# Attention and gated MLP in one kernel: the program is recorded first, then list-scheduled and pinned on each engine

## The chip, the cores and the metric

The kernel runs on one core of one Trainium2 chip. The metric is device time in microseconds (us); lower is better. The engines are TensorE (PE; its weight loads are PEld), VectorE (DVE), ScalarE (ACT), GpSimd (POOL) and SyncE (SP), which here issues every DMA.

## What is computed

Eight batches of 576 tokens. Each has eight attention heads of width 64, with a causal mask and a bias from a running sum; their outputs side by side are the input `x` (576 x 512) of a gated MLP that mixes along the sequence:

```python
bias   = -(cum[:, :, :, None] - cum[:, :, None, :])          # cum: cumsum of max(s, 0)
scores = where(causal, -1e9, scale * q @ k.T + minimum(bias, 0))
attn   = softmax(scores) @ v                                 # 64 heads
h = gelu(x @ w_in); u, v = halves of h                       # per batch, x from its 8 heads
v_n = layernorm(v) * g_ln
gated = u * (einsum('ts,bsd->btd', w_sg, v_n) + b_sg)
out = x + gated @ w_out
```

## The kernel before

All values are fp32, and most products are made from a rounded part and a remainder ("hi" and "lo", the helper `split`: a copy on ACT, then a subtraction on POOL or DVE). The first heads are left whole (8 for the scores, 12 for the product with v), since nothing fills TensorE there yet.

**A head** goes through `scores` (tiles `sc` in PSUM, two buffers; L297 and L298, L295 for whole heads), a masked running minimum on DVE (L305, into the SBUF tiles `p`, two sets for even and odd heads), the exponential on ACT (L315), `norm` on POOL (L338), 13 transposes on TensorE (`pt`, two buffers, L377), their evacuation into `pah`/`pal`, `pbh`/`pbl`, `pdh`/`pdl` (ACT copies at L88, DVE subtracts at L93), and the product with v (`xx`, one buffer, L450, and `x`, L472). ACT and DVE add the result's two halves into `xr` (L478, L479). Before a head starts, `split_head` makes `k1` and `k2` (ACT, POOL) and SP moves pieces of them by four DMAs.

**A batch's MLP**, `ffn`, first splits `xr` into `xs` (POOL, L90 and L93), four tiles, one per two heads. Its 29 units share three PSUM buffers: five `v` (tile `vm`, L510 and L524 to L527), eight `u` (`um`, L574), eight `s` (`sm`, L589 to L593), eight `o` (`om`, L608). A `v` unit ends in a chain over ACT, DVE and POOL (gelu, then layer norm). The input weights are prepared on the way, in `part`: tiles `wbits` (L216 to L222) and `wi`, `wo` (L88, L93).

**The order** is set twice. The code calls generators at places on a line that is counted in heads (`POS`, `F0`, `ORDER`); they are sorted, and the instructions are written in that order:

```python
    while steps:
        steps.sort()
        _, _, f, args = steps.pop(0)
        f(*args)
```

Then the tile framework (L711, `schedule_with_timeline_sim=True`) gives each instruction its place on its engine by a simulation of its own, and places the buffers. Each engine runs its list strictly in order.

Of the kernel before, what the change touches and what calls it, by code (L numbers as in the profile page):

```python
# [2 lines left out]

# [6 lines left out]
F32R = mybir.dt.float32r  # L10
# [3 lines left out]
AF = mybir.ActivationFunctionType  # L14
ALU = mybir.AluOpType
# [40 lines left out]
           wu=(7.0, 10.0), ws=(9.0, 11.0), wo=(11.0, 14.0), f0=2.0, f1=9.6)  # L56


@with_exitstack
def tile_attn_gmlp(  # L60
    ctx: ExitStack,
# [14 lines left out]
    att = ctx.enter_context(tc.tile_pool(name="att", bufs=2))  # L76
    moe = ctx.enter_context(tc.tile_pool(name="moe", bufs=1))
    ps_sc = ctx.enter_context(tc.tile_pool(name="ps_sc", bufs=2, space=bass.MemoryType.PSUM))
    ps_pt = ctx.enter_context(tc.tile_pool(name="ps_pt", bufs=2, space=bass.MemoryType.PSUM))
    ps_x = ctx.enter_context(tc.tile_pool(name="ps_x", bufs=1, space=bass.MemoryType.PSUM))  # L80
    ps_m = ctx.enter_context(tc.tile_pool(name="ps_m", bufs=3, space=bass.MemoryType.PSUM))

    def eng(key):
        return [{"s": nc.scalar, "g": nc.gpsimd, "v": nc.vector}[x] for x in ENG[key]]
# [11 lines left out]

    first = []

    def later():
        return tc.issue_after(first[0].ins)  # L100
# [24 lines left out]
    dram = ctx.enter_context(tc.tile_pool(name="dram", bufs=1, space=bass.MemoryType.DRAM))  # L125
# [52 lines left out]
    for i in range(2):  # L178
        t = const.tile([66, S], F32R, name=f"q2_{i}")
# [3 lines left out]
        for it in range(5):  # L183
            t = const.tile([P, PW[it]], F32, name=f"p_{i}_{it}")
# [4 lines left out]
        t = const.tile([P, 5], F32, name=f"sum_{i}")  # L189
# [36 lines left out]
    wide = w_in.dtype != F32  # L226
# [395 lines left out]
    steps = []  # L622
# [94 lines left out]
```

## Time and profile before

| | |
|---|---|
| median of 3 runs | 832.95 us (829.35 to 833.86) |
| profiled execution | 829.98 us, its span 828.2 us |
| granted TensorE clock, mean | 0.992 |
| PE busy | 794.3 us, 96% |
| DVE, ACT, POOL busy | 597.6, 577.4, 597.6 us, 70 to 72% |

Matmuls are pipelined: the duration of one runs over the start of the next, so a busy PE can still have been held up a little. Times of a chain are us from the span's start. A wait is put down to the engine whose semaphore came last.

### The profile page before, as it was taken

Reading aid. Unit: us, or ns where it says so; the run is one execution under the profiler, and the core shown is the slowest. Engines: PE = TensorE matmul, PEld = TensorE weight load, DVE = VectorE, ACT = ScalarE, POOL = GpSimd, SP = SyncE. Lnnn points to the kernel's source line nnn. Section 1 sums busy time; section 2 is a strip of 40 time slices with the busy share of each in tenths; the row PEclk is TensorE's granted clock in tenths of the full one; section 3 lists DMA queues with packets and bytes.
Section 4 is the critical chain, followed back from the end, with each engine's and each line's share of the span. In section 5 each row is a group of like instructions: output and inputs, shape, how many; then the busy total and the mean of one; then the engine's idle time right before and its main releaser. Section 6 shows DMA issues by size and latency. Waiting matters only on the chain.

```text
span 828.2 us, 16736 instructions
## 1 busy us (share of the span) xinstructions
PE 794.3 (96%) x5161; PEld 695.6 (84%) x5161; DVE 597.6 (72%) x1806; ACT 577.4 (70%) x1620; POOL 597.6 (72%) x979
## 2 busy tenths in 40 slices
PE   6899999899999999999999999999999999998898
PEld 3455666799989998999989997899989998997798
DVE  5995468975787678966887687965897678963552
ACT  4787778875686678867787677866887678853340
POOL 4987668888677767796778777796778778782541
PEclk9999999999999999999999999999999999999999
DMA  7656553334342453444434443444434443300001
GB/s 218 193 171 183 146 136 87 95 98 115 104 106 71 128 131 86 103 122 127 118 85 105 130 132 73 113 121 109 112 101 112 122 127 87 99 25 30 27 7 58
DMA packets 69804, 89.29 MB, mean 108 GB/s; under 512 B 25954, under 2 KB 42212, under 8 KB 69716
## 3 DMA queue, kind: packets, MB, share of 16 engines
q1 hardware_dynamic: 69716, 88.23, 40.6%
q8 instruction: 41, 0.67, 0.4%
q14 instruction: 47, 0.39, 0.2%
HBM read 42.27 MB, written 9.73 MB: 63 GB/s over the span
## 4 chain that ended last, share of the span: by engine, by line
PE 73%; DVE 13%; DMA 6%; ACT 3%; issue 3%; POOL 2%; SPq 1%; DVEq 0%; POOLq 0%; ACTq 0%
PE om L608 12%; PE sm L589 11%; PE um L574 10%; PE vm L510 9%; PE xx L450 9%; PE pt L377 8%; PE sc L297 4%; PE sc L298 4%; DVE p L305 2%; DMA q<-k 2%; PE sm L593 1%; DMA xq<-xs 1%; PE sm L592 1%; DVE vm L496 1%; DVE wbits L220 1%
## 5 line engine op out<-in xcount | busy, mean ns | idle before, releaser
L338 POOL TENSOR_SCALAR p<-p,rs 128x448 f32<-128x448 f32 (+4 forms) x372 | 181.0, 500 | 30.5 <-DVE rs L321 10.9
L315 ACT ACTIVATE p<-p,mn 128x448 f32<-128x448 f32 (+4 forms) x320 | 177.9, 557 | 25.5 <-DVE mn L305 23.4
L305 DVE CUSTOM_DVE_ANT_0 p<-sc,mask 64x64 f32<-64x64 f32 (+4 forms) x320 | 126.2, 422 | 55.3 <-PE pt L377 29.6
L377 PE MATMUL pt<-ident,p 128*128 128x128 f32 (+1 forms) x832 | 136.6, 278 | 4.6 <-DVE pbl L389 2.6
L574 PE MATMUL um<-xs,wi 128*128 128x288 f32 x768 | 124.1, 303 | 4.0 <-DVE vt L548 2.0
L589 PE MATMUL sm<-ws,vn 128*128 128x288 f32 x768 | 127.1, 300 | 0.4 <-DVE u L496 0.4
L93 POOL TENSOR_TENSOR k<-raw,k 128x576 fp32r<-128x576 f32 x56 | 80.6, 1439 | 63.7 <-ACT k L88 34.1
L608 PE MATMUL om<-gt,wo 128*128 128x288 f32 x768 | 125.6, 299 | 0.0
L574 PEld LDWEIGHTS um<-xs,wi 128*128 128x128 f32 x768 | 110.0, 191 | 10.3 <-DVE u L496 3.2
L377 PEld LDWEIGHTS pt<-ident,p 128*128 128x128 f32 (+1 forms) x832 | 97.0, 138 | 20.6 <-DVE pbl L389 5.4
L608 PEld LDWEIGHTS om<-gt,wo 128*128 128x128 f32 x768 | 110.5, 188 | 2.6 <-DVE ot L612 0.3
L589 PEld LDWEIGHTS sm<-ws,vn 128*128 128x128 f32 x768 | 109.9, 189 | 2.6 <-DVE u L496 1.5
L510 PE MATMUL vm<-wi,xs 128*128 128x512 f32 x384 | 105.5, 407 | 4.4 <-DVE u L496 2.2
L297 PE MATMUL sc<-k,q 128*128 128x448 f32 x336 | 100.7, 308 | 1.4 <-DVE mn L305 0.8
L298 PE MATMUL sc<-k,q 66*128 66x448 f32 x336 | 89.2, 298 | 0.4 <-DMA k<-cum 0.3
L88 ACT CAST pbh<-pt 128x512 fp32r<-128x512 f32 x104 | 49.0, 479 | 58.1 <-PE pt L377 58.0
L510 PEld LDWEIGHTS vm<-wi,xs 128*128 128x128 f32 x384 | 71.6, 194 | 20.8 <-DVE u L496 2.4
L93 POOL TENSOR_TENSOR gt<-u,gt 128x288 fp32r<-128x288 f32 x64 | 50.9, 807 | 44.3 <-ACT gt L88 43.9
L93 DVE TENSOR_TENSOR pbl<-pt,pbh 128x512 fp32r<-128x512 f32 x104 | 56.6, 549 | 16.8 <-ACT pbh L88 16.7
L297 PEld LDWEIGHTS sc<-k,q 128*128 128x128 f32 x336 | 60.6, 180 | 9.1 <-DVE mn L305 3.6
L298 PEld LDWEIGHTS sc<-k,q 66*128 66x128 f32 x336 | 60.7, 181 | 5.9 <-issue 0.8
L88 ACT CAST k<-raw 128x576 fp32r<-128x576 f32 x56 | 37.6, 671 | 38.8 <-PE sc L297 33.3
(142 smaller groups left out, 1703.2 us busy)
## 6 DMA issues: line engine op xcount, KB each, us to landing
q<-k SPq DMA_DIRECT2D x168, 144.0 KB
raw<-in_kq SPq DMA_DIRECT2D x56, 288.0 KB
vr<-in_vp SPq DMA_DIRECT2D x52, 192.0 KB
out_t<-ot SPq DMA_DIRECT2D x64, 144.0 KB
k<-k SPq DMA_DIRECT2D x56, 144.0 KB
wraw<-in_w_in SPq DMA_DIRECT2D x16, 256.0 KB
kf<-in_kq SPq DMA_DIRECT2D x8, 288.0 KB
qf<-in_kq SPq DMA_DIRECT2D x8, 288.0 KB
```

Of the source, the lines that this page charges most:

```text
L88: nc.scalar.copy(out=hi, in_=src)
L93: eng_lo.tensor_tensor(out=lo, in0=src, in1=hi.bitcast(F32), op=ALU.subtract)
L297: nc.tensor.matmul(o, d["q1"][:, i0:i0 + r], d["k1"][:, j0:j1], start=True, stop=False)
L298: nc.tensor.matmul(o, q2[h % 2][:, i0:i0 + r], d["k2"][0:66, j0:j1], start=False, stop=True)
L305: nc.vector.tensor_tensor_reduce(out=pbuf[h % 2][it][0:r, j0:j1], in0=pst[0:r, c0:c0 + j1 - j0], in1=(mask2 if it in (2, 4) else mask)[0:r ...
L315: nc.scalar.activation(out=p, in_=p, func=AF.Exp, bias=d["mn"][0:r, it:it + 1], scale=-1.0, accum_out=sums[h % 2][0:r, it:it + 1])
L338: e.tensor_scalar(out=po, in0=pi, scalar1=f, scalar2=1.0, op0=ALU.mult, op1=ALU.mult)
L377: nc.tensor.transpose(out=ps[0:n, c:c + P], in_=pb[it][:, jb:jb + n], identity=ident)
L510: nc.tensor.matmul(ps[0:r], xs[c][:, xi, ts_], wi[:, c, wj, fs], start=(n == 0), stop=(n == 11))
L574: nc.tensor.matmul(ps[:, 0:CH], wi[:, c, wj, dt * P:(dt + 1) * P], xs[c][:, xi, cs], start=(n == 0), stop=(n == 11))
L589: nc.tensor.matmul(ps[:, 0:CH], vn[j][:, vi, ds_], ws[:, j, wj, cs], start=(n == 0), stop=False)
L608: nc.tensor.matmul(ps[:, 0:CH], wo[:, c, wj, ms], gt[ch, c][:, gi, :], start=(n == 0), stop=(n == 11))
```

## The change

The kernel's mathematics, its instructions (9,712 in both, without waits and register moves) and its tables `POS`, `F0`, `ORDER` are the same. What the body calls is no longer the framework but recorders: `Pool.tile` gives a lazy tile, `Engine` notes each call in a list. When the body has run, `graph` derives which operation needs which, `plan` makes a list schedule over five engines, and `emit` makes the real calls in the order of the planned starts, with an edge between each two neighbours on an engine, so that the framework keeps that order. `plan` takes, of all engines, the operation that can start first; among those of one engine that can start at the same time, the one that stands first in the recorded order (at most 48 ready ones are looked at). A buffer goes to the next tile of its tag in the recorded order, when all users of one slot are done. Durations are formulas, and each hop from one operation to a dependent one on another engine costs a latency and 100 ns.

```diff
+LATENCY = [[54, 38, 39, 80, 60], [54, 35, 33, 77, 60], [54, 34, 35, 90, 60], [55, 34, 35, 80, 60], [60] * 5]
+OVERLAP = [0, 93, 75, 25, 0]
+ISSUE = 450.0
+MARGIN = 100
...
+    def cost(self, op):
...
+                d = 0.459 * n if m.dtype == F32R else max(0.833 * n, load) + 0.833 * n
+        elif e == ACT:
+            f = kw.get("func")
+            d = (195 if not any(ps) else 166) + 0.834 * n
+            if f == AF.Exp:
+                d = 480 + 0.834 * n
...
+        elif e == DVE:
+            d = 150 + 1.045 * n
...
+        else:
+            v = (outs or big)[0]
+            d, load = 1900 + v.dims[0][1] * v.columns() * 4 / 150.0, ISSUE
+        return e, d, load, wide, lock
...
+        text = sorted(range(len(self.ops)), key=lambda i: (start[i], rank[i]))
...
+        edges = [(a, b, mybir.DependencyClass.NoSync) for seq in order for a, b in zip(seq, seq[1:])]
...
+        for a, b, kind in edges:
+            tc.add_manual_dep(real[b], real[a].name, mybir.DependencyInfo(kind, mybir.DependencyReason.DATA),
+                              reason="order")
...
+def plan(cost, pre, first, uses, order, bufs, prio, after, slack=(0, 0, 0, 0, 0), window=48):
...
+        for e in range(5):
+            cand, least = [], 1e18
+            for pr, i in ready[e][:window]:
+                if e == PE:
+                    s = max(pest + peocc, max(at[i], pest) + cost[i][2])
+                    soon = pest + peocc + 1
+                else:
+                    s = max(at[i], free[e])
+                    soon = free[e]
+                cand.append((s, pr, i))
+                least = min(least, s)
+                if s <= soon:
+                    break
...
+        if e == PE:
+            pest, peocc, end = s, d, s + d + 60
...
+            at[j] = max(at[j], s if e == ej == PE else end + LATENCY[e][ej] + MARGIN)
...
-    nc = tc.nc
-
-    const = ctx.enter_context(tc.tile_pool(name="const", bufs=1))
+    nc = Program(tc.nc)
+
+    const = Pool(ctx.enter_context(tc.tile_pool(name="const", bufs=1)), "const", 1)
...
-        _, _, f, args = steps.pop(0)
+        nc.key, _, f, args = steps.pop(0)
         f(*args)
+
+    cost, pre, new, uses, order, bufs, after = nc.graph()
+    t, start, _, seqs = plan(cost, pre, new, uses, order, bufs, range(len(cost)), after)
+    nc.emit(tc, new, uses, seqs, start)
```

All computing instructions of the new program carry one line number, L282 (the call in `emit`), so they are told apart by their tiles.

**POOL, the first head.** `wbits` and `wi` are weight preparation; `p_4_...<-p_4_...,rs` is the last wide piece of a head's `norm`, here of head 0 (`p_4_153` before, `p_4_202` now). Before:

```order
L217 TENSOR_SCALAR wbits<-wbits 128x256 x4
L93 TENSOR_TENSOR wi<-wbits,wi 128x256
L217 TENSOR_SCALAR wbits<-wbits 128x256
L93 TENSOR_TENSOR wi<-wbits,wi 128x256
L338 TENSOR_SCALAR p_2_149<-p_2_149,rs 128x320
L338 TENSOR_SCALAR p_1_148<-p_1_148,rs 128x128
L338 TENSOR_SCALAR p_4_153<-p_4_153,rs 128x576
```

Now:

```order
L282 TENSOR_SCALAR wbits<-wbits 128x256
L282 TENSOR_SCALAR p_2_126<-p_2_126,rs 128x320
L282 TENSOR_SCALAR p_1_199<-p_1_199,rs 128x128
L282 TENSOR_SCALAR p_2_126<-p_1_199,rs 64x64
L282 TENSOR_SCALAR p_3_130<-p_0_189,rs 64x64
L282 TENSOR_SCALAR p_4_202<-p_4_202,rs 128x576
```

Six of the seven weight instructions that stood ahead of head 0's `norm` now stand behind it.

**TensorE, a head of batch 3.** `p_4` in the first row is the last transpose of the head's first block, which is evacuated to `pah` and `pal`; `xx<-pah` is the first product that needs it. Before:

```order
L377 MATMUL pt<-ident,p_4_153 128x128
L297 MATMUL sc<-k_4768,q_4770 128x320
L298 MATMUL sc<-k_4769,q_0_145 128x320
L297 MATMUL sc<-k_4768,q_4770 128x192
L298 MATMUL sc<-k_4769,q_0_145 128x192
L574 MATMUL um<-xs,wi 128x288 x12
L377 MATMUL pt<-ident,p_3_151 128x128 x2
L377 MATMUL pt<-ident,p_2_149 128x128
L377 MATMUL pt<-ident,p_4_153 128x128
L589 MATMUL sm<-ws,vn 128x288 x12
L450 MATMUL xx<-pah,vs 128x512
```

Now (the first of the two `p_4` transposes is the one that ends the block, the second is of the next block):

```order
L282 MATMUL sm<-ws,vn 128x288
L282 MATMUL sc<-k_4518,q_4526 128x288
L282 MATMUL sc<-k_4530,q_0_93 128x288
L282 MATMUL pt<-ident,p_4_238 128x128 x2
L282 MATMUL um<-xs,wi 128x288 x5
L282 MATMUL xx<-pah,vs 128x512
```

Between the two stood 32 other instructions of TensorE; now there are one transpose and five matmuls.

**TensorE, the end of attention.** The last head of all writes `xx<-pdl` and `xx<-pdh`; the last MLP's `vm` needs it through `xr` and `xs`. Before:

```order
L608 MATMUL om<-gt,wo 128x288 x12
L450 MATMUL xx<-pdh,vs 128x192
L472 MATMUL x_10809<-pdh,vs 128x64
L450 MATMUL xx<-pdl,vs 128x192
L450 MATMUL xx<-pdh,vs 128x64
L510 MATMUL vm<-wi,xs 128x512 x2
L574 MATMUL um<-xs,wi 128x288
L510 MATMUL vm<-wi,xs 128x512
L574 MATMUL um<-xs,wi 128x288 x2
L510 MATMUL vm<-wi,xs 128x512 x12
```

Now, directly behind the last head:

```order
L282 MATMUL xx<-pdl,vs 128x192
L282 MATMUL xx<-pdh,vs 128x64
L282 MATMUL om<-gt,wo 128x288 x9
L282 MATMUL sm<-ws,vn 128x288 x8
L282 MATMUL sm<-wr_1045,vnr_10602 128x288
```

and, after three more `sm` units, up to the last MLP's first `vm`:

```order
L282 MATMUL sm<-ws,vn 128x288 x12
L282 MATMUL sm<-wr_1045,vnr_10602 128x288
L282 MATMUL sm<-wr_1073,vnr_109 128x288
L282 MATMUL om<-gt,wo 128x288 x24
L282 MATMUL vm<-wi,xs 128x512 x6
```

Before, `vm` followed the head at once; now 85 matmuls of the MLP before it stand between.

## Rows read from the trace of the kernel before

**Rows 1.** The page's part 1: per engine its busy time, share of the span and instructions.

```profile
PE 794.3 (96%) x5161; PEld 695.6 (84%) x5161; DVE 597.6 (72%) x1806; ACT 577.4 (70%) x1620; POOL 597.6 (72%) x979
```

**Rows 2.** Busy time of each engine in three stretches of the span (us from its start): stretch, length, busy time of PE, PEld, DVE, ACT and POOL with instruction counts, granted TensorE clock, DMA share, GB/s.

```profile
0.00:200.00 200.00, 182.65 (x964) 126.66 (x965) 144.28 (x462) 142.91 (x418) 153.59 (x240) 0.99 0.52 144
200.00:750.00 550.00, 543.37 (x3775) 506.17 (x3775) 419.26 (x1274) 412.41 (x1156) 418.45 (x690) 1.00 0.41 105
750.00:828.00 78.00, 68.24 (x426) 62.81 (x424) 34.06 (x71) 22.05 (x46) 25.57 (x50) 0.93 0.10 32
```

**Rows 3.** The same table for the attention-only start and for the stretch after it.

```profile
18.00:60.00 42.00, 37.68 (x152) 19.44 (x152) 39.67 (x117) 33.03 (x102) 37.40 (x52) 0.96 0.63 197
66.00:100.00 34.00, 33.13 (x155) 19.26 (x154) 19.83 (x75) 23.95 (x73) 24.18 (x36) 1.00 0.65 175
```

**Rows 4.** The chain of work that ended last, in order of time: start us, us, what. The first matmuls of all, and the same output unit (`om`, 12 matmuls) in two batches, three batches apart.

```profile
5.89 2.57 PE cps L143 x9
...
387.98 1.61 PE om L608 x12
...
669.46 1.61 PE om L608 x12
```

**Rows 5.** The same chain in a stretch without a wait in the middle of the span: TensorE's pieces at full pace. `pt` is four transposes, `xx` one product of 512 columns, `vm` twelve of 512, `sc` one each of 448, 320 and 192.

```profile
386.39 0.49 PE pt L377 x4
...
390.02 0.23 PE xx L450
...
393.46 2.79 PE vm L510 x12
...
396.57 0.20 PE sc L298
...
397.09 0.15 PE sc L298
...
397.33 0.11 PE sc L298
```

**Rows 6.** The same chain around 410 us, where it leaves TensorE: a split of k on POOL, two transfers, the SP queue (SPq) between them.

```profile
409.94 0.62 POOL k L93
...
410.96 4.00 DMA q<-k
...
415.28 0.64 SPq L520
...
415.97 3.83 DMA xq<-xs
...
419.84 0.50 PE vm L524
```

**Rows 7.** Instructions grouped by line, engine, tile and shape: xcount | busy us, mean ns of one | idle time of the engine just before them and what ended it. Weight preparation on POOL and DVE, an exponential on ACT with the read-out of its sum, the two halves of a split out of PSUM.

```profile
L217 POOL TENSOR_SCALAR wbits<-wbits 128x256 f32<-128x256 f32 x24 | 21.2, 891 | 9.5 <-ACT wbits L216 9.1
L93 POOL TENSOR_TENSOR wi<-wbits,wi 128x256 fp32r<-128x256 f32 x16 | 12.8, 806 | 1.5 <-ACT wi L88 1.4
L315 ACT ACTIVATE p<-p,mn 128x576 f32<-128x576 f32 x64 | 49.6, 775 | 3.0 <-DVE mn L305 2.9
L315 ACT ACTIVATION_READ_ACCUMULATOR p<-p,mn 128x1 f32 x256 | 48.3, 189 | 0.0
L88 ACT CAST pah<-pt 128x512 fp32r<-128x512 f32 x52 | 30.5, 587 | 1.2
L93 DVE TENSOR_TENSOR pal<-pt,pah 128x512 fp32r<-128x512 f32 x52 | 35.6, 686 | 16.0 <-ACT pah L88 16.0
```

**Rows 8.** Waits between 12 and 100 us: who waited for whom, us in total, times, longest.

```profile
PEld sc L295 <- DVE mn L305: 7.6, 10, 1.9
PE sc L295 <- DVE mn L305: 4.3, 6, 1.4
```

**Rows 9.** TensorE's timeline at its three waits after 750 us: start us, us, instruction, in brackets the idle time before it and who ended it.

```profile
760.77 0.80 PE L510 MATMUL vm<-wi,xs 128*128 128x512 f32 x1 [2.15 <-POOL xs L90]
...
778.06 1.22 PE L510 MATMUL vm<-wi,xs 128*128 128x512 f32 x2 [2.21 <-DVE u L496]
...
787.99 1.27 PE L574 MATMUL um<-xs,wi 128*128 128x288 f32 x4 [2.01 <-DVE vt L548]
```

**Rows 10.** The chain over the first of these waits: from the last head's result in PSUM to the split tile `xs`.

```profile
758.65 0.59 ACT xr L478
...
759.26 0.69 DVE xr L479
...
760.04 0.68 POOL xs L90
```

**Rows 11.** The stretches around these waits; columns as in the windows above, the granted clock third from the right.

```profile
758.00:765.00 7.00, 4.82 (x18) 3.67 (x18) 2.41 (x5) 2.25 (x6) 2.08 (x2) 0.76 0.06 21
775.00:783.00 8.00, 5.79 (x22) 4.52 (x21) 3.58 (x8) 3.31 (x8) 5.43 (x10) 0.79 0.07 17
783.00:790.00 7.00, 4.99 (x27) 4.34 (x25) 5.55 (x11) 3.98 (x8) 1.73 (x8) 0.86 0.01 2
```

**Rows 12.** TensorE's timeline at one transpose that stands alone between matmuls.

```profile
736.21 0.29 PE L593 MATMUL sm<-wr,vnr 66*128 66x288 f32 x1
736.34 0.27 PE L377 MATMUL pt<-ident,p 128*128 128x128 f32 x1
736.37 0.77 PE L608 MATMUL om<-gt,wo 128*128 128x288 f32 x4
```

More of the change, by code (lines that the diff above doesn't have):

```diff
@@ L1 @@
-from contextlib import ExitStack
+from bisect import bisect_left, insort
+from contextlib import ExitStack, contextmanager
 from itertools import count
@@ L56, with __init__, make @@
            wu=(7.0, 10.0), ws=(9.0, 11.0), wo=(11.0, 14.0), f0=2.0, f1=9.6)
+PE, ACT, DVE, POOL, SP = range(5)
+METHODS = {"tensor": PE, "scalar": ACT, "vector": DVE, "gpsimd": POOL, "sync": SP}
+LATENCY = [[54, 38, 39, 80, 60], [54, 35, 33, 77, 60], [54, 34, 35, 90, 60], [55, 34, 35, 80, 60], [60] * 5]
+OVERLAP = [0, 93, 75, 25, 0]
+ISSUE = 450.0
+MARGIN = 100
+class Buf:
+    def __init__(self, pool, shape, dt, name, tag, bufs):
+        self.pool, self.shape, self.dt, self.name, self.bufs = pool, list(shape), dt, name, bufs
+        self.tag = (pool.name, tag or (name, pool.serial()))
+        self.named = tag
+        self.real = None
+    def make(self):
+        if self.real is None:
+            kw = {"name": self.name}
+            if self.named:
+                kw.update(tag=self.named, bufs=self.bufs)
+            self.real = self.pool.real.tile(self.shape, self.dt, **kw)
+        return self.real
@@ new lines, with __init__, step, __getitem__ @@
+class View:
+    def __init__(self, buf, dims, off, dt, how):
+        self.buf, self.dims, self.off, self.dtype, self.how = buf, dims, off, dt, how
+    def step(self, dims, off, how, dt=None):
+        return View(self.buf, dims, off, dt or self.dtype, self.how + [how])
+    def __getitem__(self, key):
+        ks = key if isinstance(key, tuple) else (key,)
+        dims, off = [], list(self.off)
+        for n, (s, c) in enumerate(self.dims):
+            k = ks[n] if n < len(ks) else slice(None)
+            a, b = (k, k + 1) if isinstance(k, int) else (k.start or 0, c if k.stop is None else k.stop)
+            off[n == 0] += a * (1 if n == 0 else s)
+            if n == 0 or not isinstance(k, int):
+                dims.append((s, b - a))
+        return self.step(dims, off, lambda x: x[key])
+    def rearrange(self, text, **kw):
+        dims = self.dims
+        if "(" in text:
+            n = 1
+            for _, c in dims[1:]:
+                n *= c
+            dims = [dims[0], (dims[-1][0], n)]
+        return self.step(dims, self.off, lambda x: x.rearrange(text, **kw))
+    def bitcast(self, dt):
+        return self.step(self.dims, self.off, lambda x: x.bitcast(dt), dt)
+    def columns(self):
+        n = 1
+        for _, c in self.dims[1:]:
+            n *= c
+        return n
+    def span(self):
+        lo = self.off[0]
+        return (self.off[1], self.off[1] + self.dims[0][1], lo,
+                lo + 1 + sum(s * (c - 1) for s, c in self.dims[1:]))
+    def make(self):
+        x = self.buf.make()
+        for f in self.how:
+            x = f(x)
+        return x
@@ new lines, with __init__, serial, tile @@
+class Pool:
+    count = 0
+    def __init__(self, real, name, bufs, psum=False, dram=False):
+        self.real, self.name, self.bufs, self.psum, self.dram = real, name, bufs, psum, dram
+    def serial(self):
+        Pool.count += 1
+        return Pool.count
+    def tile(self, shape, dt, name=None, tag=None, bufs=None):
+        b = Buf(self, shape, dt, name, tag, bufs or self.bufs)
+        dims, s = [], 1
+        for c in reversed(shape):
+            dims.insert(0, (s, c))
+            s *= c
+        return View(b, dims, [0, 0], dt, [])
@@ new lines, in plan, with put, grant @@
+def plan(cost, pre, first, uses, order, bufs, prio, after, slack=(0, 0, 0, 0, 0), window=48):
+    n = len(cost)
+    left = [len(p) for p in pre]
+    succ = [[] for _ in range(n)]
+    for i, p in enumerate(pre):
+        for q in p:
+            succ[q].append(i)
+    issue = [[] for _ in range(n)]
+    for i, qs in after.items():
+        for q in qs:
+            issue[q].append(i)
+            left[i] += 1
+    owner, remain = {}, {}
+    for i in range(n):
+        for b in first[i]:
+            owner[b] = i
+            left[i] += 1
+        for b in uses[i]:
+            remain[b] = remain.get(b, 0) + 1
+    ready = [[] for _ in range(5)]
+    at = [0.0] * n
+    tagof = {b: t for t, bs in order.items() for b in bs}
+    free_slots = {t: [0.0] * bufs[t] for t in order}
+    nxt = {t: 0 for t in order}
+    last = {}
+    def put(j):
+        left[j] -= 1
+        if left[j] == 0:
+            insort(ready[cost[j][0]], (prio[j], j))
+    def grant(t):
+        while free_slots[t] and nxt[t] < len(order[t]):
+            b = order[t][nxt[t]]
+            nxt[t] += 1
+            f = free_slots[t]
+            x = min(f)
+            f.remove(x)
+            j = owner[b]
+            at[j] = max(at[j], x)
+            put(j)
+    for i in range(n):
+        if left[i] == 0:
+            insort(ready[cost[i][0]], (prio[i], i))
+    for t in order:
+        grant(t)
+    free = [0.0] * 5
+    start, fin = [0.0] * n, [0.0] * n
+    pest = peocc = 0.0
+    held = asked = (0.0, 0.0)
+    seqs = [[] for _ in range(5)]
+    for _ in range(n):
+        best = None
+        for e in range(5):
[4 more added lines that the diff above has]
+                    soon = pest + peocc + 1
+                else:
+                    s = max(at[i], free[e])
[4 more added lines that the diff above has]
+                    break
+            for c in cand:
+                if c[0] <= least + slack[e]:
+                    if best is None or c[0] < best[0]:
+                        best = (c[0], e, c[1], c[2])
+                    break
+        if best is None:
+            return None
+        s, e, pr, i = best
+        del ready[e][bisect_left(ready[e], (pr, i))]
+        _, d, load, wide, lock = cost[i]
+        if e == PE:
+            pest, peocc, end = s, d, s + d + 60
+            free[e] = s
+        elif e == SP:
+            free[e], end = s + load, s + d
+        else:
+            if e == DVE and wide and held[0] <= s < held[1]:
+                s = held[1]
+            if e == POOL and lock and asked[0] <= s < asked[1]:
+                s = asked[1]
+            end = s + d
+            if wide:
+                asked = (s, end)
+            if lock:
+                held = (s, end)
+            free[e] = end - OVERLAP[e]
+        start[i], fin[i] = s, end
+        seqs[e].append(i)
+        for j in issue[i]:
+            at[j] = max(at[j], s)
+            put(j)
+        for j in succ[i]:
+            ej = cost[j][0]
+            at[j] = max(at[j], s if e == ej == PE else end + LATENCY[e][ej] + MARGIN)
+            put(j)
+        for b in uses[i]:
+            remain[b] -= 1
+            last[b] = max(last.get(b, 0.0), end)
+            if remain[b] == 0:
+                free_slots[tagof[b]].append(last[b] + 60)
+                grant(tagof[b])
+    return max(fin), start, fin, seqs
@@ L97, in tile_attn_gmlp @@
     first = []
+    @contextmanager
     def later():
-        return tc.issue_after(first[0].ins)
+        nc.gate = first[0]
+        yield
+        nc.gate = None
     def load(h):
@@ L122, in load @@
                 nc.sync.dma_start(out=d["vr"], in_=vp[h])
[L125 removed]
+    dram = Pool(ctx.enter_context(tc.tile_pool(name="dram", bufs=1, space=bass.MemoryType.DRAM)), "dram", 1, dram=True)
     cum = dram.tile([2, BH, S], F32, name="cum")
```

124 lines of the change are left out of this document (118 added, 6 removed).

## Prediction

> **What bounds the kernel now.** I read the engines' shares first, then busy time by stretch, then the chain of waits, then the single waits. TensorE is busy 96% of the span, the others 70 to 72% [rows 1]. A matmul's recorded duration runs into the next one's, so this share hides small hold-ups; two readings give their size. First, plain idle time: TensorE idles 200 - 182.65 = 17.4 us in the first 200, 550 - 543.4 = 6.6 in the next 550 and 78 - 68.2 = 9.8 in the last 78 [rows 2]. Second, pace: three batches take 669.46 - 387.98 = 281.5 us, 93.8 each [rows 4]. At full pace a column costs 0.46 ns (12 x 288 in 1.61 us, 12 x 512 in 2.79, 448 in 0.20) and a transpose 0.49/4 = 0.12 us [rows 4, 5]. A head has 3,200 columns of scores and 3,072 of products with v, 2.9 us, and 13 transposes, 1.6 us: 4.5 us, 36 for eight. The MLP has 24 units of 1.61, 16 single matmuls of 0.134 in the `s` units, four `v` units of 2.79 and a fifth of 8 x 0.23: 53.8 us. So 89.8 of 93.8 us are work, and 4.0 per batch, 23 us in the middle 550, are not. One of these places is seen whole: TensorE waits for `xq`, whose transfer stood in SP's queue behind one that itself waited for a split of k [rows 6].
>
> In the first stretch TensorE shares the bound: from 18 to 60 us POOL is busy 37.4 and DVE 39.7 of 42 us, and TensorE 37.7; from 66 to 100 POOL and DVE have 10 us or more to spare [rows 3].
>
> **The change part by part.** Instructions, transfers and program order stay; only the order on each engine moves. The sum is made against the profiled execution, 830.0 us (span 828.2 and 1.8 around it), which lies 3 us under the median of 832.95.
>
> *Start.* POOL prepares weights at 0.891 and 0.806 us per instruction [rows 7]. Counted in the orders, 5 of the first and 2 of the second kind stood ahead of head 0's `norm`, 6.1 us, and one stands there now, 0.9 us; ahead of the fourth head's it was 15 and 12 (23.0 us) and is 8 and 5 (11.2 us). So where POOL is full, early heads come 5 to 12 us of POOL time sooner. The work isn't gone: by the thirteenth head both orders have done the same number. What can be won is TensorE's idle time alone: 17.4 us less the 5.9 before the first matmul [rows 4], 11.5, in which the waits for the two score buffers lie (7.6 and 4.3 us, some of it under running matmuls) [rows 8]. I take 8, nearer that end because POOL was relieved of about that much. The other end: the first `v` units, whose weights now come later, wait as long as POOL was relieved at head 0, 5 us slower.
>
> *Middle.* Of the 23 us the new order can win those that come from a fixed place in a queue, as at `xq`: the last MLP input now lies some 17 us of TensorE work further ahead of the first `vm` (counted in the orders at the pace above), so SP's delay there is covered. Against it, hand-overs are tighter. Between the end of a head's first block and `xx<-pah` TensorE had 2 x 0.15 + 2 x 0.1 + 12 x 0.134 + 4 x 0.12 + 12 x 0.134 = 4.2 us of other work; now it has 0.12 + 5 x 0.134 = 0.79 us. Needed are the transpose's run-out, 0.27 - 0.12 = 0.15 [rows 12], the ACT copy, 0.587 [rows 7], and two semaphores: nothing is left over. Counted over all split heads the median of this lead falls from 4.1 to 1.2 us. I take 11 us won and 0.1 us lost at one hand-over in each of 52 heads, 5: net 6. Ends: 23 won, and 0 (the losing end is the first rival).
>
> *End.* After the last head `vm` waited 2.15 us [rows 9] for two copies into `xr` and the split, 0.59 + 0.69 + 0.68 [rows 10]. Now 85 matmuls stand there, 85 x 0.134 = 11.4 us: covered. [...] The first wait goes with its clock, 3.9. The second and third (2.21 and 2.01 us [rows 9]) are for PSUM buffers that the `v` units' chain over ACT and DVE holds; the last `vm`s stand as before, but the first two start earlier, so I take 2 of the second. Sum 6; ends 0 and 6.4 + 4.4 = 10.8.
>
> *Nothing, and why.* The planner's durations are those of the rows: 166 + 0.834 x 512 = 593 ns for the copy that took 587, 685 for the subtract of 686, 480 + 0.834 x 576 = 960 for an exponential of 775 + 189 [rows 7]. Its transfers are too fast: 1900 + 147,456/150 = 2,883 ns where 4.00 us was seen [rows 6]. The cover is that a head's k is split after the head two before it is done with the buffer, and the order leaves at least 10.2 us of TensorE work from there to its first use (9.2 before); without it, 1.1 us per head.
>
> *Switches.* The orders have 249 runs of transposes before and 406 now. A lone transpose costs no more than one in a run: from its start to the end of the four matmuls behind it are 0.80 us, of which 3 x 0.134 + 0.29 = 0.69 are the matmuls', so 0.11 against 0.12 [rows 5, 12]. I cost the 157 new runs at nothing. [...]
>
> Sum: 8 + 6 + 6 = 20, **810 us**.
>
> **The rivals.** *Hand-overs decide (slower).* Every block of transposes (four per head, 208 in the split heads) now returns just in time; if ACT or DVE is late, TensorE stands, and in-order queues pass it on. At 0.15 us per block this costs 31 us: 841. The point is (20 + 4)/208 = 0.12 us per block. For it: 0.79 us of lead against 0.74 needed. Against it: ACT and DVE idle 28 to 30% [rows 1], the durations agree, and the plan adds 0.1 us to each hop.
>
> *New waits for old (no change).* The early heads gain but the `v` units give it back, the middle trades one wait for another, and the end wins its 2.15: 828.
>
> *Nearly all of it goes.* 11.5 + 17 + 10: 792. For it: the planner looks at all five engines with measured durations. Against it: many of the 4 us per batch are gaps too small to have one cause.
>
> [...]
>
> *The order isn't kept.* The framework still places buffers and waits; were its slots taken late, nothing would be won: 830. The built order shows the planned neighbours, so this is little.
>
> **How the numbers follow.** Forecast 0.54, nearly all 0.13, new waits 0.14, hand-overs 0.15, switches 0.02, order not kept 0.02. A measurement can tell about 0.5%, 4.2 us, from no change: 828.8 to 837.1. Faster by more: 0.54 + 0.13 and a little of the 828 case, 0.68. Slower: 0.15 + 0.02, 0.17. Within: 0.15. The range reaches from half-way between the forecast and the 792 case, to which unequal parts of both ends belong, to the hand-over case at 0.13 to 0.14 us per block: 795 to 838, with about 0.1 left out on each side.
>
> **What would show it.** Start: head 0's `norm` on POOL several us earlier, and less idle of TensorE in the first 200 us than 17.4. Middle: more than 93.8 us per batch would mean the hand-overs decide, with `xx` waiting for ACT `pah` or `pbh` in the list of waits; 92 to 93 is the forecast. End: no wait of `vm` for POOL `xs`, and the first stretch with clock 1.0; the buffer waits still there. Switches: a lone transpose well above 0.12 us. The prediction is wrong if the middle gets longer, or if TensorE's idle time at the start stays while POOL is relieved.

## The result: 1% slower, and the profile after

The changed kernel takes 838.83 us (median of 7; 835.90 to 840.14) beside 830.08 for the kernel before (median of 7): ratio 1.0093, 95% interval 1.0068 to 1.0119. Forecast were 810 and a range from 795 to 838. The profiled execution has a span of 837.4 us, 9.2 more than that of before.

The shares of the changed kernel look as before; TensorE does the same 5,161 instructions [rows 1]:

```profile
PE 798.2 (95%) x5161; PEld 699.0 (83%) x5161; DVE 600.2 (72%) x1806; ACT 578.0 (69%) x1620; POOL 594.3 (71%) x979
```

By stretch, to be read beside [rows 2, 3] (third from the right is the granted clock):

```profile
0.00:200.00 200.00, 178.07 (x924) 127.35 (x924) 138.26 (x443) 136.91 (x398) 147.98 (x233) 0.94 0.50 137
200.00:750.00 550.00, 541.30 (x3699) 497.03 (x3697) 422.83 (x1283) 416.02 (x1169) 412.87 (x688) 1.00 0.42 107
750.00:838.00 88.00, 78.80 (x544) 74.58 (x542) 39.09 (x82) 25.07 (x54) 33.48 (x60) 1.00 0.10 32
...
18.00:60.00 42.00, 35.80 (x140) 18.97 (x140) 27.09 (x94) 26.88 (x84) 28.96 (x43) 0.88 0.50 150
66.00:100.00 34.00, 34.00 (x172) 21.57 (x173) 26.78 (x85) 29.79 (x90) 27.95 (x40) 1.00 0.66 175
100.00:200.00 100.00, 90.26 (x550) 74.45 (x548) 71.68 (x219) 69.43 (x196) 80.21 (x129) 0.93 0.41 103
```

TensorE idles 21.9 us of the first 200 (17.4 before), and the clock share fell from 0.99 to 0.94. POOL, filled in the start before, has a third of the 42 us from 18 to 60 free: it was relieved, and TensorE idles more all the same.

To see when the time went, I count each recorded matmul at a fixed price (the 30th percentile of start to next start of its tile and shape in the kernel before, 115 ns for a transpose; 753.8 us in all for both) and sum what has started by a moment. "TensorE's work" below means this.

| by | 100 us | 200 | 400 | 750 | last matmul |
|---|---|---|---|---|---|
| before | 75.8 | 163.9 | 357.5 | 692.7 | 824.9 |
| changed | 78.1 | 157.7 | 344.1 | 677.1 | 834.1 |
| ahead | +2.3 | -6.2 | -13.4 | -15.6 | -9.2 |

Won: 2.3 up to 100 us and 6.4 after 750. Lost: 8.5 from 100 to 200 and 9.4 from there to 750, most of it by 400.

**What stands in the start.** The waits for the score buffers, which the prediction meant to win [rows 8], are nearly gone: 0.6 us from 12 to 100, where they were 4.3. In their place TensorE waits for transfers, 9.8 us from 12 to 200 against 0.3 before; the largest of them (in all, times, longest):

```profile
PE sc L282 <- DMA kf<-cf: 4.2, 2, 2.3
PE sc L282 <- DMA q<-k: 3.8, 1, 3.8
PE sc L282 <- DMA k<-k: 1.3, 2, 1.0
```

One of them in full is the chain at 16 us: scores wait for a key tile (`kf`), for which the plan has 3.9 us and the chip took 5.60, then for a row of 2.2 KB behind it on SP (2.62, with 1.9 planned):

```profile
16.05 5.60 DMA kf<-in_kq
21.65 0.02 issue
21.67 2.62 DMA kf<-cf
24.28 0.14 issue
```

TensorE stands with transposes queued behind that matmul (five, from 26.05 us on), so DVE runs dry; its timeline (idle time in brackets):

```profile
24.04 0.42 DVE L282 SCALAR_TENSOR_TENSOR wbits<-wraw,wbits 128x256 int32<-128x256 int32 x1
27.36 0.55 DVE L282 COPY pdh<-pt 64x64 f32<-64x64 f32 x2 [2.90 <-PE pt L282]
32.37 0.62 DVE L282 CUSTOM_DVE_ANT_0 p<-sc,mask 128x448 f32<-128x448 f32 x1 [4.46 <-PE sc L282]
```

Then the deferred weights come due. POOL's work on `wbits` in two stretches, before:

```profile
50.00:100.00 50.00, 10.73 (x13) 1.00 0.59 161
100.00:130.00 30.00, 0.00 (x0) 1.00 0.47 114
```

and changed:

```profile
50.00:100.00 50.00, 15.28 (x19) 1.00 0.61 166
100.00:130.00 30.00, 5.97 (x7) 0.89 0.62 158
```

From the thirteenth head on POOL also splits `vs`, from the ninth `k`. At 147 us two weight pieces stand ahead of a split of `k`, and the transfers that bring its result to `q` hang behind it. POOL, then TensorE:

```profile
146.90 0.89 POOL L282 TENSOR_SCALAR wbits<-wbits 128x256 f32<-128x256 f32 x1
...
147.91 0.85 POOL L282 TENSOR_SCALAR wbits<-wbits 128x256 f32<-128x256 f32 x1
...
148.87 1.42 POOL L282 TENSOR_TENSOR k<-raw,k 128x576 fp32r<-128x576 f32 x1
```

```profile
149.32 1.95 PE L282 MATMUL um<-xs,wi 128*128 128x288 f32 x13
155.03 0.59 PE L282 MATMUL sc<-k,q 128*128 128x448 f32 x2 [3.76 <-DMA q<-k]
156.52 0.90 PE L282 MATMUL pt<-ident,p 128*128 128x128 f32 x3 [0.90 <-POOL p L282]
```

The plan itself holds this wait: it starts the matmuls before and after it at 124.9 and 128.8 us, and the run was hardly later after it (26.2 us) than before (26.1).

**The end.** TensorE's waits after 750 us, beside [rows 9]: that for `xs` is gone; the two for PSUM buffers stay, 1.42 and 1.86 us long where they were 2.21 and 2.01; those of 0.94 and 0.70 are new. The granted share of the 16 us from 752 on is 1.00, where [rows 11] had 0.76 at the first wait.

```profile
776.32 1.66 PE L282 MATMUL vm<-wi,xs 128*128 128x512 f32 x6 [0.94 <-DVE ot L282]
789.95 3.06 PE L282 MATMUL vm<-wi,xs 128*128 128x512 f32 x12 [1.42 <-DVE u L282]
798.30 1.85 PE L282 MATMUL um<-xs,wi 128*128 128x288 f32 x12 [1.86 <-DVE vt L282]
802.32 0.77 PE L282 MATMUL um<-xs,wi 128*128 128x288 f32 x4 [0.70 <-DVE vt L282]
```

```profile
752.00:768.00 16.00, 16.00 (x121) 15.81 (x120) 6.92 (x16) 4.73 (x12) 8.26 (x10) 1.00 0.08 27
```

### The profile page after: what moved, and what is told of

It is laid out like the page before. It is cut to its first block, busy times and chain, and to the rows that moved or that the text cites. A ratio compares the mean times of both kernels' runs of the same rounds, so it can differ in the third digit from the quotient of the medians.

```text
span 837.4 us, 16785 instructions
## 1 busy us (share of the span) xinstructions
PE 798.2 (95%) x5161; PEld 699.0 (83%) x5161; DVE 600.2 (72%) x1806; ACT 578.0 (69%) x1620; POOL 594.3 (71%) x979
## 4 chain that ended last, share of the span: by engine, by line
PE 76%; ACT 8%; DVE 6%; DMA 3%; POOL 3%; issue 2%; SPq 1%; POOLq 0%; DVEq 0%; ACTq 0%
PE sm L282 12%; PE om L282 12%; PE xx L282 11%; PE vm L282 11%; PE sc L282 11%; PE pt L282 10%; PE um L282 8%; ACT p L282 2%; ACT vt L282 1%; ACT u L282 1%; DMA k<-k 1%; DVE vm L282 1%; DVE p L282 1%; ACT vn L282 1%; POOL vs L282 1%
## 5 line engine op out<-in xcount | busy, mean ns | idle before, releaser
L282 ACT ACTIVATE p<-p,mn 128x448 f32<-128x448 f32 (+4 forms) x320 | 178.1, 558 | 33.1 <-DVE mn L282 31.3
L282 POOL TENSOR_SCALAR p<-p,rs 128x448 f32<-128x448 f32 (+4 forms) x372 | 179.5, 492 | 27.6 <-DVE rs L282 9.7
L282 PE MATMUL pt<-ident,p 128*128 128x128 f32 (+1 forms) x832 | 163.1, 283 | 9.3 <-POOL p L282 5.6
L282 DVE CUSTOM_DVE_ANT_0 p<-sc,mask 128x448 f32<-128x448 f32 (+4 forms) x320 | 125.1, 420 | 40.9 <-PE sc L282 32.4
L282 PE MATMUL sc<-k,q 66*128 66x288 f32 (+9 forms) x672 | 137.1, 312 | 8.8 <-DMA q<-k 3.8
L282 PE MATMUL sm<-ws,vn 128*128 128x288 f32 x768 | 139.1, 307 | 1.2 <-DVE u L282 0.6
L282 PE MATMUL um<-xs,wi 128*128 128x288 f32 x768 | 136.6, 305 | 3.3 <-DVE vt L282 2.6
L282 PEld LDWEIGHTS pt<-ident,p 128*128 128x128 f32 (+1 forms) x832 | 102.9, 140 | 38.8 <-POOL p L282 11.0
L282 PE MATMUL om<-gt,wo 128*128 128x288 f32 x768 | 129.3, 303 | 0.0
L282 PE MATMUL vm<-wi,xs 128*128 128x512 f32 (+1 forms) x416 | 126.8, 410 | 2.4 <-DVE u L282 1.4
L282 PEld LDWEIGHTS sc<-k,q 128*128 128x128 f32 (+3 forms) x672 | 103.5, 182 | 22.2 <-DMA q<-k 4.0
L282 PEld LDWEIGHTS um<-xs,wi 128*128 128x128 f32 x768 | 113.6, 191 | 9.8 <-DVE vt L282 3.0
L282 PEld LDWEIGHTS sm<-ws,vn 128*128 128x128 f32 x768 | 113.6, 190 | 2.6 <-DVE u L282 1.1
L282 PEld LDWEIGHTS om<-gt,wo 128*128 128x128 f32 x768 | 109.6, 189 | 0.9
L282 POOL TENSOR_TENSOR k<-raw,k 128x576 fp32r<-128x576 f32 x56 | 79.8, 1425 | 32.8 <-ACT k L282 30.7
L282 PEld LDWEIGHTS vm<-wi,xs 128*128 128x128 f32 (+1 forms) x416 | 73.3, 188 | 13.8 <-DVE u L282 1.8
L282 POOL TENSOR_TENSOR gt<-u,gt 128x288 fp32r<-128x288 f32 x64 | 50.8, 807 | 41.4 <-ACT gt L282 41.4
L282 POOL TENSOR_TENSOR vs<-vr,vs 128x384 fp32r<-128x384 f32 x52 | 53.3, 1025 | 37.6 <-ACT vs L282 35.5
L282 DVE SCALAR_TENSOR_TENSOR u<-u,um 128x288 f32<-128x288 f32 x128 | 56.6, 443 | 12.8 <-ACT u L282 12.0
L282 DVE TENSOR_TENSOR pbl<-pt,pbh 128x512 fp32r<-128x512 f32 x104 | 56.8, 549 | 10.0 <-ACT pbh L282 9.7
L282 DVE SCALAR_TENSOR_TENSOR ot<-om,xr 128x288 f32<-128x288 f32 x64 | 29.2, 456 | 46.5 <-PE om L282 43.3
L282 ACT CAST pbh<-pt 128x512 fp32r<-128x512 f32 x104 | 50.1, 482 | 15.4 <-PE pt L282 14.8
```

The source lines that it names most:

```text
L282: r = getattr(op["eng"].real, op["name"])(*[f(a) for a in op["args"]], **{k: f(v) for k, v in op["kw"].items()})
```

## Experiments

The plan works out a start for every instruction, so each run can be compared with its own plan. The changed kernel's plan ends at 800.2 us; the chip took 837.4. In brackets behind a time stand its ratio to the kernel before, run beside it, and the 95% interval. Theories: A, transfers are planned too short; B, hops between engines are; C, switches between transposes and matmuls cost; O, the order costs, not the machinery (P); A2, several prices are short and one alone mended doesn't help; F, it is the price of full-precision matmuls.

**1. Transfers and margin**, one at a time (the first two edits, or the last) and together. A control changes the margin to 110.

```diff
-ISSUE = 450.0
+ISSUE = 600.0
-            d, load = 1900 + v.dims[0][1] * v.columns() * 4 / 150.0, ISSUE
+            d, load = 3100 + v.dims[0][1] * v.columns() * 4 / 150.0, ISSUE
-MARGIN = 100
+MARGIN = 200
```

> The planner's price of a transfer is raised from 1,900 to 3,100 ns plus bytes/150, and of an issue on SP from 450 to 600; everything else as in the change. Theory A (transfers: the plan counted on data that lands 0.7 to 1.8 us later than planned, so SP's in-order queue and the scores stand at places where the plan saw none): the plan itself now ends at 818 instead of 800, and its own arithmetic, run over the fixed order with these prices and no margin, gives 809 where the changed kernel's order gives 831; with some clock lost at waits I expect 812 to 820 on the chip, under the kernel before, and TensorE's waits for transfers gone. Theory B (hand-overs among the engines are planned too tight): the margin is unchanged, so no gain, 835 to 842. Theory C (switches between transposes and matmuls cost): 389 runs of transposes against 406, so no gain, 835 to 842.

> Only the planner's margin per hop between engines is raised from 100 to 200 ns; transfers are priced as in the change. Theory A (transfers): no help; its waits stay and the looser order wins nothing, 835 to 850 (the plan's arithmetic with slower transfers gives 847 against 831). Theory B (hand-overs): faster by ten us or more, 815 to 828. Theory C (switches): 400 runs of transposes against 406, 835 to 842.

> Both edits: transfers at 3,100 ns plus bytes/150, issue 600, and margin 200. Theory A: as with the transfers alone, within 5 us of that run (the plan's arithmetic gives 809 for both). Theory B: clearly faster than the run with the transfers alone, by 10 us or more. Theory C: 396 runs of transposes, 835 to 842.

> The change with a margin of 110 ns instead of 100, which should mean nothing by itself: a control of how much the planned order's time moves when the list scheduling falls out otherwise (its plan ends at 800.8 instead of 800.2). Theory A2: still slow, 833 to 845. If one planned order is as good as a draw from a wide spread, it may come out at 820 or 850.

Measured: transfers alone 849.49 (1.0233; 1.0183 to 1.0284), margin alone 853.20 (1.0262; 1.0214 to 1.0311), both 833.34 (1.0034; 1.0007 to 1.0061), margin 110 841.48 (1.0168; 1.0135 to 1.0202). A and B, each by itself, fall: either edit made it slower by over 10 us. C falls with the runs below: an order with 405 runs of transposes takes 828.48 us (section 4) and one with 262 takes 844.26 (section 2). By 200 us the run with both was 4.3 us of TensorE's work ahead of the kernel before, those with one edit 4.6 and 6.7 behind; by 750 us the run with both was 7.7 behind as well. In the one control, 10 ns of margin moved the time by 3 us and the ratio from 1.0093 to 1.0168, so up to about 6 us between two planned orders need not come from the price that was changed.

TensorE's waits from 12 to 200 us say why one edit alone doesn't help:

| order | for transfers, us | for engines, us |
|---|---|---|
| before | 0.3 | 10.7 |
| change | 9.8 | 6.4 |
| transfers | 0.7 | 13.5 |
| margin 200 | 3.2 | 9.8 |
| both | 0.0 | 10.3 |

With the dearer transfers the waits for them go, and TensorE waits for POOL, ACT and DVE instead; only with both are the two as short as before.

**2. The framework orders from the planned text**, without the pinning edges.

```diff
-        edges = [(a, b, mybir.DependencyClass.NoSync) for seq in order for a, b in zip(seq, seq[1:])]
+        edges = []
```

> The planned order is given out as the text of the program, but without the edges that pin neighbours on each engine, so the framework's own scheduler orders the engines from it. If the plan's order as such costs the time (theories A to C), this comes back to near the kernel before, 825 to 838, as far as the framework undoes it; if the pinning is what helps and the text order is poor, it is slower than the change, over 842.

844.26 us (1.0165; 1.0116 to 1.0213). The framework made another order of it (262 runs of transposes against 406), so the run gives no answer as to the cause; that pinning isn't the harm is shown by the next section.

**3. The old order on the new machinery, and one part of the plan at a time.** The five orders of the kernel before are written into the file; `splice` holds the operations that aren't `free` to them (in issue order on each engine), and the planner places the rest. `free` is nothing, the first 2,000 operations, those from 8,500, and those from 2,000.

```diff
+    new, after = splice(nc, cost, pre, uses, lambda i: i >= 8500)
     t, start, _, seqs = plan(cost, pre, new, uses, order, bufs, range(len(cost)), after)
```

> The changed kernel's machinery (recorded program, own order given out, pinned on each engine) with the order of the kernel before on all five engines instead of the planned one. Theory O (what the planned order does costs the time, not how it is given out): as the kernel before, 827 to 833. Theory P (the pinning, the order of the text or the buffers placed from it cost): near the change, 836 to 842. By the plan's own arithmetic this order ends at 824, close to the 828 that the kernel before took; the planned one ends at 800 and took 837.

> The first 2,000 operations of the program (about the first 180 us: weights and the first heads) are placed by the planner, all others keep the order of the kernel before among themselves. Theory O with the loss in the start: by 280 us the changed kernel was 9.0 us of TensorE work behind the kernel before, so this one takes 834 to 842. If the loss of the start comes only with the order of what follows, 826 to 832. By the plan's arithmetic it should win 12: 815 to 820 if that holds.

> Only the last 810 operations (from number 8,500, about the last 100 us) are placed by the planner, all before them keep the order of the kernel before. The step of the prediction on the end gave 6 us, and the changed kernel made up 6.4 us of TensorE work after 750 us: 821 to 826. If that was only the same work shifted from before 750 us, 828 to 833.

> The first 2,000 operations keep the order of the kernel before, the planner places all after them: the middle and the end of the change without its start. The changed kernel lost 6.6 us of TensorE work between 280 and 750 us and won 6.4 after. If the middle's order costs by itself: 826 to 833, 4 to 8 above the run with the end alone. If the middle only lost through what the start left it: 821 to 826, as with the end alone.

| planned | us | ratio, interval |
|---|---|---|
| nothing | 828.71 | 0.9992 (0.9967 to 1.0018) |
| start | 844.50 | 1.0174 (1.0150 to 1.0198) |
| end | **823.94** | **0.9924 (0.9894 to 0.9954)** |
| middle and end | 830.77 | 1.0015 (0.9997 to 1.0032) |

The machinery costs nothing (P falls). The planned end wins 5.9 us and beats both kernels. The planned middle costs 6.8 beside it. The start alone costs 15: 6.0 us of TensorE's work by 200 us and 8.9 more from 200 to 280, at the seam, where the old order takes over from the planned start. In section 5 the seam at the same place costs 8.3, 6.5 and 6.8 in three runs and 1.2 in the fourth. That the old order doesn't fit what such a start leaves is my reading, not shown; by it the start's own share is the 6.

How the middle loses: from 271 to 649 us a batch takes 94.3 to 94.9 us with it planned; in the old order, between the same units, 92.6 to 93.6. The same waits come back in every batch, here with middle and end planned:

```profile
618.93 0.33 PE L282 MATMUL pt<-ident,p 128*128 128x128 f32 x1 [0.51 <-POOL p L282]
...
637.43 0.53 PE L282 MATMUL sc<-k,q 128*128 128x288 f32 x2 [0.70 <-DVE mn L282]
```

Between 300 and 740 us TensorE waited 2.6 us for POOL `p` and 2.5 for DVE `mn` there; in the old order for neither. As other waits are shorter there, plain idle time grew by about 2 us in these 440; the rest lies in hold-ups too short to show, which I can't name.

**4. The price of a full-precision matmul.** In [rows 4, 5] I had taken only the fast ones. These are the first heads' products with v, clock 1.00, in the kernel before (start to next start: 1.00 us for 512 columns, 1.44 for 448 and 320, 0.47 for 192, 0.26 for 64, and as much for the last):

```profile
95.92 1.07 PE L450 MATMUL xx<-pal,vf 128*64 128x512 f32 x2
96.92 0.52 PE L377 MATMUL pt<-ident,p 128*64 128x128 f32 x3
97.37 1.50 PE L450 MATMUL xx<-pbl,vf 128*64 128x448 f32 x4
98.81 0.40 PE L297 MATMUL sc<-k,q 128*128 128x288 f32 x1
...
99.53 0.54 PE L450 MATMUL xx<-pdh,vf 128*64 128x192 f32 x2
100.00 0.33 PE L468 MATMUL xx<-pdh,vf 64*64 64x64 f32 x2
100.26 0.33 PE L469 MATMUL x<-pdh,vf 128*64 128x64 f32 x2
```

The plan has 0.85, 0.75 + 0.53, 0.32, 0.11 and 0.11: 0.76 us short per head. With 120 such matmuls (those of the whole heads' scores among them), 110 ns each, this is 13 us of TensorE. The price depends on what stands around: in the changed kernel the head at 106.53 us is 0.6 short.

```diff
-                d = 0.459 * n if m.dtype == F32R else max(0.833 * n, load) + 0.833 * n
+                d = 0.459 * n if m.dtype == F32R else max(0.833 * n, load) + 0.833 * n + 110
```

The second run also sets 2500 and 600 for transfers and a margin of 150.

> The change with one price mended: a matmul at full precision costs the plan 110 ns more (about 120 such matmuls in the first 12 heads, 13 us of TensorE). Transfers and margin as in the change. Theory F (this price is the main error in the start): the plan now ends at 811 instead of 800; the order no longer counts on TensorE being there too early, so the run lags its plan by under 20 us, not 37, and takes 820 to 830, with TensorE's work at 200 us level with the kernel before. Theory A2 (transfers and hops): no change, 835 to 843.

> The same price and half of the other two: transfers 2,500 ns plus bytes/150, issue 600, margin 150 ns. The plan ends at 818. Theory F: within 6 us of the run with that price alone. Theory A2: clearly below it, 822 to 832. A planned order that loses its gain to any looseness: 825 to 835.

837.26 us (1.0100; 1.0068 to 1.0132), and 828.48 (1.0000; 0.9985 to 1.0015). F alone falls too. A2 is what the runs bear out: with all three prices raised, transfers and margin by half only, 10 us come back. Whether all three are needed isn't shown, as no run raises the full-precision price with one other alone. In the second run the weights are prepared earlier on POOL (`wbits`, as above):

```profile
50.00:100.00 50.00, 20.38 (x25) 1.00 0.59 158
100.00:130.00 30.00, 1.58 (x2) 1.00 0.39 94
```

The lag of the runs behind their own plans (median of TensorE's instructions planned for 200 to 212 us, and the span less the plan's end) puts it together:

| order | plan ends | lag at 200 | span | lag at the end |
|---|---|---|---|---|
| old | 823.9 | 4.8 | 826.6 | 2.7 |
| change | 800.2 | 29.6 | 837.4 | 37.2 |
| margin 110 | 800.8 | 30.2 | 840.8 | 40.0 |
| margin 200 | 822.0 | 27.7 | 855.0 | 33.0 |
| transfers | 818.4 | 20.0 | 847.7 | 29.3 |
| full precision | 811.2 | 18.2 | 835.4 | 24.2 |
| all three (section 4) | 818.1 | 8.7 | 827.0 | 8.9 |
| transfers and margin | 824.6 | 12.1 | 829.4 | 4.8 |

The plan's arithmetic is right for the old order to 3 us, and 37 short for the order made by it; 24 of these are there by 100 us. My reading is that the list scheduler put each instruction where the model saw it fit, so that every price that is too short was used up. In the plan's arithmetic, with the orders as they stand, 110 ns per full-precision matmul make the old order 1.6 us longer and the planned one 13.2. And with transfers and margin both raised the plan promises 824.6, no better than the 823.9 of the old order in the plan as it was.

The raised prices aren't simply the true ones. With the dearer transfers (margin 100) the same arithmetic gives 870.5 us for the old order, which took 826.6 on the chip. So either these prices are too dear or its 823.9 holds by errors that offset each other, and the runs don't tell whether raised prices help because they are nearer the truth or because they keep dependent instructions further apart.

**5. Joining a better start to the old middle.** In order: the start planned with the dearer transfers; with these and margin 200; the same and the end; start and end with the full-precision price; the same with the seam moved from operation 2,000 to 4,000.

> As the run with the planned start (first 2,000 operations placed by the planner, the rest in the order of the kernel before), with the dearer transfers alone (3,100 ns plus bytes/150, issue 600). Theory A2 (the start loses because transfers and hops are both planned too short, and either mended alone is not enough): by 200 us the run with the dearer transfers on the whole program was still 4.6 us of TensorE work behind, so 832 to 842. Theory A (transfers alone): 822 to 829.

> The same with both prices raised: transfers 3,100 ns plus bytes/150, issue 600, margin 200 ns per hop. Theory A2: by 200 us the run with both on the whole program was 4.3 us of TensorE work ahead of the kernel before; if what follows in the old order can keep it, 822 to 829, if the seam costs it, 829 to 834. If a planned start loses whatever the prices: 836 to 846.

> Both prices raised, the first 2,000 and the last 810 operations placed by the planner, the middle in the order of the kernel before. If the gains add: the run before this one less the 6 us of the end alone, 816 to 824 by theory A2. If not, the end alone stays the best, 824.

> The full-precision price mended, the first 2,000 and last 810 operations planned, the middle in the order of the kernel before. Theory F and no loss at the seam: 815 to 822, below the end alone (824). With the 6 to 9 us that the seam cost in the runs before: 824 to 832. Theory A2: 834 to 840.

> The same with the seam moved from operation 2,000 to 4,000, into the steady middle where weights are done. If the seam's cost came from the weights and first heads being in another state than the old order assumes, it is gone here: 815 to 824 by theory F. If any join costs, 826 to 834.

843.79 (1.0191; 1.0153 to 1.0230), 833.15 (1.0058; 1.0041 to 1.0076), 827.16 (1.0002; 0.9975 to 1.0028), 831.26 (1.0026; 1.0000 to 1.0051) and 835.84 (1.0098; 1.0078 to 1.0117). Both prices are worth 11 us in the start alone (844.50 to 833.15; 10 by the ratios), the transfers by themselves 0.7: A2 again. With both, TensorE's work is level with before at 200 us (164.5 against 163.9), and 5.8 behind at 280: the seam. The end's gain adds to it in full (833.15 to 827.16). Moving the seam to 4,000 settles nothing: with the full-precision price alone, TensorE was 7.3 us behind by 200 and lost only 1.2 at the seam at 2,000. None beats the end alone. A start with all three prices, joined to the old middle, was not run.

Taken together, though some of these starts are alike, they leave little to chance: by 200 us the nine orders whose planned start had none or one of the prices raised are 4.6 to 7.8 us of TensorE's work behind the kernel before, the four with two or three raised 0.7 to 4.3 ahead.

**6. Middle and end with the prices of section 4.**

> As the run with the old start and everything after operation 2,000 planned (830.8), with all three prices of the run that came to 828.5: full-precision matmuls 110 ns more, transfers 2,500 ns plus bytes/150, issue 600, margin 150. If the middle lost its 7 us against the end alone through short prices: 822 to 826, the end's gain alone. If the planner's rule (first in program order whenever ready) makes a middle that is worse by itself: 828 to 834.

> As the run with the planned end alone (823.9), with the same three prices. If the end's gain stands on its order (the last heads' attention earlier, waits covered by other work) and not on prices: 821 to 826 again. If it leaned on the prices: 826 to 832.

833.13 (1.0048; 1.0030 to 1.0066) and 824.34 (0.9944; 0.9924 to 0.9964). The end's gain doesn't lean on the prices, and raising them doesn't mend the middle. What is left is the planner's rule (first in program order as soon as ready), but this is argued, not shown: no run changes the rule.

## Why the prediction was wrong, step by step

- **Start, +8: -6.2 by 200 us.** The step that failed is "the planner's durations are those of the rows", and with it the cover for the transfers. I compared a copy, a subtract and an exponential, saw that transfers were planned too short and called them covered, and didn't look at full-precision matmuls. The idle time that the sum meant to win did go where it lay, at the score buffers, and POOL was relieved as forecast (the first wide piece of head 0's `norm` starts at 19.11 us, before at 22.40). But 9.8 us of waits for transfers came in its place, and TensorE idles 21.9 us, not less than 17.4, which the prediction had named as a sign of being wrong. The 10.2 us of cover from a `k` split to its use didn't hold at 155 us, where POOL came to the split late. No single price repairs the start; two or three together do (sections 1, 4, 5).
- **The clock in the start, put at nothing.** The sum counted clock at the end only. Over the first 200 us the granted share fell from 0.99 to 0.94; while TensorE was working this cost 10.0 us of full-speed time, before 1.6. This is more than the 6.2 us that were lost by then.
- **The weights.** "The work isn't gone" was given no price, and it came due between 100 and 130 us beside the `k` splits. No run takes the weights alone, so their share is read from traces, not shown.
- **Middle, +6: -9.4** from 200 to 750, 6.8 by experiment. A batch takes 94.3 us from 377 on, where the forecast had 92 to 93; a longer middle was the other sign named. Of 4 us per batch I took half to be waits for places in a queue. `xq`'s wait was only 2.0 us in these 550, and 0.4 in the old order run again; it went, and others took its place. The lead of `xx` that I feared (ACT `pah`, `pbh`) isn't among the waits: what is late is `p` from POOL at the transposes, 2.6 us, and scores, 1.7 for `mn` and 1.5 for one transfer. Waits explain some 2 us of the loss; the cause of the rest stays open.
- **End, +6: +6.4**, and 5.9 by experiment. Right in mechanism: the wait is covered, its clock is back, buffer waits are left. The size is partly luck. I counted some 4 us of waits and 1.7 of clock. No run shows the 1.7 in the sum's 3.9, nor the 4.4 in its upper end, as a time of its own; the shares of [rows 11] give them, as (1 - 0.76) x 7 = 1.7, (1 - 0.79) x 8 = 1.7 and (1 - 0.86) x 7 = 1.0. TensorE's waits after 750 us fell by 1.3 only (6.6 to 5.3, as new ones came), but the clock stayed up at all of them: the share rose from 0.93 over 78 us, which is 5.5 us, to 1.00.
- **Switches, 0:** right, as far as these rows and the runs under C show. Single transposes in the changed kernel: two of 192 columns, each followed by one, take 0.32 us, of which 0.18 are columns:

```profile
598.26 0.25 PE L282 MATMUL xx<-pdh,vs 128*128 128x192 f32 x1
598.35 0.27 PE L282 MATMUL pt<-ident,p 128*128 128x128 f32 x1
598.38 0.34 PE L282 MATMUL xx<-pdl,vs 128*128 128x192 f32 x1
598.55 0.27 PE L282 MATMUL pt<-ident,p 128*128 128x128 f32 x1
598.58 0.28 PE L282 MATMUL xx<-pdh,vs 128*128 128x64 f32 x1
```

That is 0.07 us for each, under the 0.12 of one in a row. The 0.02 that the forecast gives to switches is for a cost at each new run of transposes; no run shows it: these two took 0.07 us each, and an order with 405 runs took 828.48 us (section 4), as much as the kernel before (1.0000).
- **Rivals.** "Hand-overs decide" had the sign but not the place, so that its 841 lies near the 839 measured is luck. That an order could be worse than its own plan by 37 us, through prices, was none of them. "New waits for old" is what the start and the middle did, at a loss.

## What to carry to other kernels

An order made from a model leans on every price in it that is too short; that the model gives the old order's time says nothing on the new one's. Before believing a plan, compare each kind of instruction of each stage with a row, the rare ones of the start too, and ask how late the plan may run before it stalls. Count the clock with each wait that TensorE gets: here it was 10 us in the first 200. Then try the parts of a new order apart: here the last 810 of 9,310 operations held the whole gain.

## What the runs showed of the hardware

In or just after each of TensorE's longest waits between 20 and 200 us of the changed kernel (2.32, 1.86, 1.63 and 3.76 us) the granted clock fell for 3.4 to 6.8 us. Its records hold the shares 1.00 and 0.50 only (0.50 in each us from 23 to 29, 1.00 in each from 30 to 36); the mean shares of the stretches of 8 us below lie between these two. Here it fell at the wait of 2.32 us from 22 us on, in the waits from 112 on (1.02 and 1.63 us), and after the one of 3.76 that ends at 155.

```profile
24.00:32.00 8.00, 7.58 (x22) 3.56 (x22) 1.01 (x5) 2.26 (x7) 5.08 (x9) 0.65 0.15 52
112.00:120.00 8.00, 5.17 (x21) 4.09 (x22) 7.47 (x23) 5.75 (x17) 5.53 (x10) 0.68 0.74 204
152.00:160.00 8.00, 4.06 (x20) 3.76 (x21) 6.22 (x15) 4.06 (x11) 7.34 (x13) 0.79 0.44 123
```

These three stretches alone lose (0.35 + 0.32 + 0.21) x 8 = 7.0 us of full-speed time, 5.8 of them while TensorE was working, beside the waits (the kernel before lost 0.18 x 8 = 1.4 in the first and none in the others); over the whole run the mean share fell from 0.992 to 0.984.

Full-speed time lost is counted here as the missing share times the length. In the kernel before, twelve products of 288 columns that ran almost wholly at 0.50 took 790.98 - 787.99 = 2.99 us from the first start to the next instruction's, where twelve take 1.61 at full pace [rows 4]; by this pair a us at 0.50 loses 0.46 us, not 0.50, so the sums are a little too high.

```profile
787.99 3.19 PE L574 MATMUL um<-xs,wi 128*128 128x288 f32 x12 [2.01 <-DVE vt L548]
790.98 1.19 PE L589 MATMUL sm<-ws,vn 128*128 128x288 f32 x6
```

What it is worth shows within one order: of the four runs with the full-precision price alone (section 4), three had a mean share of 0.988 to 0.990 and took 837.07 to 838.30 us, and one had 1.000 and took 832.54. The profiled runs of the nine orders whose planned start had none or one of the prices raised have 0.972 to 0.990; the two with several raised throughout, 0.998 and 0.995.
